# One addition and one fp32 product for a norm's sum over heads, and the second exponential of a visit ahead of its FFN group

## The chip, the cores and the metric

The kernel runs on one core of one Trainium2 chip. The metric is device microseconds of one launch. Most runs of a kernel agree within about 0.3%. A timed run is about 1.8 us longer than the span of its profile, which goes from the first to the last instruction.

## The reference

Blockwise causal attention on `q, k, v` of shape (8, 8, 576, 64), then an RMS norm and a SwiGLU FFN on the 4608 tokens of 512 features:

```python
attn = softmax(scale * q @ k.T, masked by blocks of 64)        # per head
x    = (attn @ v) with heads side by side                      # 4608 x 512
rms  = sqrt(mean(x * x, axis=-1) + 1e-06)
xn   = x / rms * rms_g
g, val = xn @ w_gate, xn @ w_val                               # 512 -> 1536
out  = (g * (1 / (1 + exp(-g))) * val) @ w_out                 # 1536 -> 512
```

## The kernel before

It treats attention batch by batch and lays the FFN's groups between attention's steps, in the order in which the program was written, so that TensorE always has products to do.

**An FFN group** (up). Eight products fill two PSUM buffers, ScalarE takes a tanh of the first, and VectorE makes `gs` and then `HT`. The buffer of `g` comes free with `gs`, that of `u` with `HT`. All FFN groups, norms and value products share four such buffers, in turn.

```python
g = ps_f.tile([P, TOKC], FP32, name="fps")        # ps_f has 4 buffers
u = ps_f.tile([P, TOKC], FP32, name="fps")
...                                               # 4 + 4 matmuls of 128x512 (line 502)
nc.scalar.activation(out=th, in_=g, func=AF.Tanh, scale=0.5)                    # line 506
nc.vector.scalar_tensor_tensor(out=gs, in0=th, scalar=1.0, in1=g, ...)          # line 508
nc.vector.tensor_mul(out=HT[n][:, m:m + k, lo:lo + w], in0=gs..., in1=u...)     # line 510
```

**The norm** of a batch, as a chain of small VectorE operations on 18 columns: a transpose `tr`, reciprocal, two products `w`, then for batches 2 to 7 the sum over heads, split into three bf16 terms whose products with a constant matrix are added in PSUM. A chain of nine more operations (from `ve`), the product `S` and a transpose give the spread norm `st`.

```python
nc.vector.tensor_add(out=rest[:, 0:n], in0=w2[:, 0:n, 0], in1=w2[:, 0:n, 1])   # line 388
for i in range(3):
    nc.vector.tensor_copy(out=term[:, i, 0:n], in_=rest[:, 0:n])               # line 391, a cast
    if i < 2:
        nc.vector.tensor_sub(out=rest[:, 0:n], in0=rest[:, 0:n], in1=term[:, i, 0:n])
...
for i, x in enumerate(terms):
    nc.tensor.matmul(ms[:, 0:n], GSUM if len(terms) == 2 else GSUMB, x, ...)   # line 401
```

**A visit** to attention, batches 3 to 7: two scores products (each into one of two PSUM buffers), the value products of pairs that are complete, and between one and three FFN groups. The number of groups is 1 in only four visits, all in batch 3. I number batch 3's visits from 0; those four are 0, 2, 4 and 6.

```python
es = [scores_mm(*x) if x[2] is not None else scores_ends_mm(x[0]) for x in two]
if len(complete) > 1:
    values_of_two()
...
for n in range(max(1, int(want) - given)):
    if es:
        scores_exp(*es.pop(0))
    group()
    given += 1
for e in es:
    scores_exp(*e)
```

**Corners.** Causal blocks need a 64 x 64 corner of an exponential set to zero. `scores_exp` notes it, and `clear()` at the end of `group()` writes the zeros.

The softmax here doesn't subtract the row's maximum and nothing guards it: scores larger than these inputs give would overflow.

Of the kernel before, what the change touches and what calls it, by code (L numbers as in the profile page):

```python
# [9 lines left out]
FP32 = mybir.dt.float32  # L10
BF16 = mybir.dt.bfloat16
# [6 lines left out]
def kernel(  # L18
# [11 lines left out]
    nc = tc.nc  # L30
# [4 lines left out]
    P = 128  # L35
# [6 lines left out]
    NSUB = S // 32  # L42
# [25 lines left out]
    const = ctx.enter_context(tc.tile_pool(name="const", bufs=1))  # L68
# [8 lines left out]
    small = ctx.enter_context(tc.tile_pool(name="small", bufs=1))  # L77
# [19 lines left out]
    SEL = const.tile([P, 7, 32], BF16, name="SEL")  # L97
    SELB = const.tile([P, HP, P], BF16, name="SELB")
    GSUM = const.tile([P, P], FP32, name="GSUM")
    GSUMB = const.tile([P, P], BF16, name="GSUMB")  # L100
    gscale = const.tile([P, HP], FP32, name="gscale")


# [68 lines left out]
    for t in range(HP):  # L172
        for a in range(2):
            r = 32 * t + a
            nc.vector.tensor_copy(out=SELB[:, t, a * D:(a + 1) * D],
                                  in_=ident[:, r:r + 1].to_broadcast([P, D]))
# [3 lines left out]
    for i in range(4):  # L180
        nc.gpsimd.affine_select(
            out=GSUM.rearrange("p (j i) -> p j i", j=4), in_=GSUM.rearrange("p (j i) -> p j i", j=4),
# [41 lines left out]
    def clear():  # L224
        while corners:
            nc.vector.memset(corners.pop(0)[1], 0.0)
# [9 lines left out]
    def scores_mm(b, t, step):  # L236

        if step in (0, "a"):
            PT[b, t] = ppool.tile([P, 2, PW], BF16, name="PT")
        sp = ps_s.tile([P, 2, 512], FP32, name="sps")  # L240
        for c, q0, w, o in STEPS[step][0]:
            for a in range(2):
                r = slice(a * D, (a + 1) * D)
                nc.tensor.matmul(sp[:, a, o:o + w], KT[b][r, t, c * P:(c + 1) * P],  # L244
                                 QT[b][r, t, q0:q0 + w], start=True, stop=True,
                                 skip_group_check=True)
        return (b, t), sp, step

    def scores_exp(pair, sp, step):

        if step is None:
            nc.scalar.activation(out=P4[pair].rearrange("p a t d -> p a (t d)"),
                                 in_=sp[:, :, 0:HP * BLK], func=AF.Exp, scale=SCALE)
            return
        parts, lo, width = STEPS[step]
        pt = PT[pair]
        nc.scalar.activation(out=pt[:, :, lo:lo + width], in_=sp[:, :, 0:width],  # L257
                             func=AF.Exp, scale=SCALE)
        for c, q0, w, o in parts:
            if c and q0 == c * P:  # L260
                corners.append((pair, pt[BLK:P, :, lo + o:lo + o + BLK]))
# [66 lines left out]
    nrm = {}  # L328
# [42 lines left out]
            o += w  # L371
        nrm[key] = tr, o

    def norm_ratio(key, split=False):
        tr, width = nrm[key]
        n = width // 32
        tv = tr.rearrange("p (s r) -> p s r", r=32)
        rec = small.tile([P, NSUB, 2], FP32, name="rec")
        nc.vector.reciprocal(out=rec[:, 0:n], in_=tv[:, 0:n, 0:2])
        w2 = small.tile([P, NSUB, 2], FP32, name="w2")  # L380
        nc.vector.tensor_mul(out=w2[:, 0:n], in0=tv[:, 0:n, 2:4], in1=rec[:, 0:n])
        nc.vector.tensor_mul(out=w2[:, 0:n], in0=w2[:, 0:n], in1=rec[:, 0:n])
        if not split:
            nrm[key] = (rec, [w2[:, 0:n, 0], w2[:, 0:n, 1]], n)
            return

        rest = small.tile([P, NSUB], FP32, name="ws")
        nc.vector.tensor_add(out=rest[:, 0:n], in0=w2[:, 0:n, 0], in1=w2[:, 0:n, 1])
        term = small.tile([P, 3, NSUB], BF16, name="wt")
        for i in range(3):  # L390
            nc.vector.tensor_copy(out=term[:, i, 0:n], in_=rest[:, 0:n])
            if i < 2:
                nc.vector.tensor_sub(out=rest[:, 0:n], in0=rest[:, 0:n], in1=term[:, i, 0:n])
        nrm[key] = (rec, [term[:, i, 0:n] for i in range(3)], n)

    def norm_root(key):

        rec, terms, n = nrm[key]
        ms = ps_f.tile([P, 512], FP32, name="fps")
        for i, x in enumerate(terms):  # L400
            nc.tensor.matmul(ms[:, 0:n], GSUM if len(terms) == 2 else GSUMB, x,
                             start=(i == 0), stop=(i == len(terms) - 1))
        ve = small.tile([P, NSUB], FP32, name="ve")
        nc.vector.tensor_scalar_add(out=ve[:, 0:n], in0=ms[:, 0:n], scalar1=EPS)
        sh = small.tile([P, NSUB], I32, name="sh")
        nc.vector.tensor_single_scalar(sh[:, 0:n], ve[:, 0:n].bitcast(I32), 1,
                                       op=ALU.logical_shift_right)
        y = small.tile([P, NSUB], FP32, name="y0")
        nc.vector.tensor_scalar(out=y[:, 0:n].bitcast(I32), in0=sh[:, 0:n], scalar1=-1,
                                scalar2=0x5f3759df, op0=ALU.mult, op1=ALU.add)  # L410
        nrm[key] = (rec, ve, y, n)
# [102 lines left out]
    def ffn_down(n, i):  # L514
        eng = nc.gpsimd if n < NTC - 2 else nc.sync
        rows = []
        for j in range(2):
            blk = (n * TOKC + i * P) // BLK + j
            b, pos = divmod(blk, S // BLK)
            rows.append(b * S + ((pos + 1) % (S // BLK)) * BLK)  # L520
        osb = obuf.tile([P, DM], FP32, name="osb")
        last = (n, i) == downs[-1]
        step = DM // 2 if last else DM
        for o in range(0, DM, step):
            po = ps_f.tile([P, DM], FP32, name="fps")
            for m in range(NMC):
                nc.tensor.matmul(po[:, 0:step], HT[n][:, m, i * P:(i + 1) * P],  # L527
                                 WO[:, m, o:o + step], start=(m == 0), stop=(m == NMC - 1))
            nc.scalar.mul(out=osb[:, o:o + step], in_=po[:, 0:step], mul=0.5)  # L529
            if rows[1] == rows[0] + BLK:  # L530
                eng.dma_start(out=out[rows[0]:rows[0] + P, o:o + step], in_=osb[:, o:o + step])  # L531
            else:
                for j in range(2):
                    e = nc.scalar if last and j else eng
                    e.dma_start(out=out[rows[j]:rows[j] + BLK, o:o + step],  # L535
                                in_=osb[j * BLK:(j + 1) * BLK, o:o + step])
# [19 lines left out]
    def group(n=1):  # L556

        nonlocal ui, di, gone
        for _ in range(n):
            dn, dt = downs[di] if di < len(downs) else (0, 0)  # L560
            have = NMC * (dn + 1) if dn or dt > 1 else NMC // 2
            ready = di < len(downs) and have <= ui
            up = ui < len(ups) and ups[ui][0] * TOKC + ups[ui][3] + ups[ui][4] <= ready_x
            far = ui - NMC
            if ready and have + 2 <= ui and far >= DOWN0 and (ui == len(ups) or 3 * di <= far - 3):
                ffn_down(*downs[di])
                di += 1
            elif up:
                ffn_up(*ups[ui])
                ui += 1  # L570
            elif ready:
                ffn_down(*downs[di])
                di += 1
            clear()
            gone += 1
            now = [d for d in due if d[0] <= gone]
            due[:] = [d for d in due if d[0] > gone]
            for _, fn, args in now:
                fn(*args)
# [18 lines left out]
    def late_tail(b):  # L598
        norm_sums(b, b, WHOLE)
        norm_squares(b, b, WHOLE)  # L600
        norm_turn(b)
        norm_ratio(b, True)
        later(2, norm_root, b)
        later(2, norm_newton, b, 0)
        later(3, norm_newton, b, 1)
        later(3, norm_spread, b)
        later(3, norm_copies, b)
        for t in range(HP):
            later(9 + t // 2, norm_apply, b, t)
        later(10, mark, b * S + S)  # L610
# [79 lines left out]
    later(2, norm_newton, "b", 1)  # L690
    later(2, norm_spread, "b")

    nc.vector.tensor_copy(out=GSUMB, in_=GSUM)


    group()
    transpose_pair(1, 0, on_act="qk")
# [73 lines left out]
    want = given = 0  # L771
# [12 lines left out]
    for i in range(0, len(steps), 2):  # L784
        two = steps[i:i + 2]
        if sums:
            late_tail(sums.pop())
# [3 lines that stand above are left out]
        complete += [x[0:2] for x in two if x[2] == 2]  # L791
        b = two[0][0]
        want += 10 / 6.5 if b == 3 else 16 / 6.5
        for n in range(max(1, int(want) - given)):
            if es:
                scores_exp(*es.pop(0))
            group()
            given += 1
        for e in es:
            scores_exp(*e)  # L800
        fetch(b + 1, 2)
    group()
    values_of_two()
# [34 lines left out]
```

## Time and profile before

| | before |
|---|---|
| median of all runs at the prediction | 392.32 us (392.03 to 392.41) |
| span of the profile | 392.3 us |
| TensorE busy, VectorE busy, ScalarE busy | 95%, 68%, 48% |
| small operations of a split, each from start to start | 0.21 us |

TensorE sets the time, so a change elsewhere counts only where TensorE waits. The views are shown in the prediction (the number in brackets is idle time before the line, with what ended it). This profile had a slow start. Here TensorE waits for batch 0's values at 14 us (the number in brackets is idle time before the line, with what ended it):

```profile
15.92 0.22 PE L299 MATMUL fps<-PT,VB 128*64 128x64 bf16 x2 [1.49 <-DMA VB<-in_v_dram]
```

The trace also shows the clock granted to TensorE at half from 16.12 to 19.53 us; the changed kernel's trace shows no such stretch at the start. The profiled run took 394.07 us, 1.8 above the median of the timed ones. So two profiles can be compared only from a common point behind the start. I use the end of the fourth output copy on ScalarE, at 78.51 us in this trace.

### The profile page before, as it was taken

How to read it: one execution, taken by the hardware profiler on the slowest of the kernel's cores; microseconds unless marked ns; L12 is line 12 of the kernel's file. 1: busy time of each engine (PE TensorE's matmuls, PEld its weight loads, DVE VectorE, ACT ScalarE, POOL GpSimd, SP SyncE). 2: the span in 40 equal slices, each digit the busy share in tenths (PEclk: the TensorE clock that was granted, in tenths of full speed). 3: DMA queues.
4: the chain of work that ended last, by engine and by line, in shares of the span. 5: the costliest groups of instructions: out<-in, count | busy, mean ns of one | idle time of the engine just before them, and what ended most of it. 6: DMA issues, size and time to landing. Idle time of an engine off the chain costs nothing.

```text
span 392.3 us, 7763 instructions
## 1 busy us (share of the span) xinstructions
PE 374.6 (95%) x3017; PEld 182.4 (46%) x3056; DVE 265.1 (68%) x651; ACT 189.6 (48%) x270; POOL 128.7 (33%) x181
## 2 busy tenths in 40 slices
PE   7779999999999999999999999999999999999996
PEld 3457666433434444444444444444444444444443
DVE  4678668377887788368977686488776847554430
ACT  3733883277555645465566445546542323332322
POOL 8826864756117402494030742400100110100000
PEclk9899999999999999999999999999999999999999
DMA  7999999999919918999961999802100220100113
GB/s 99 166 203 195 184 154 156 154 178 164 166 38 112 133 22 139 166 113 137 134 102 11 78 179 160 131 1 74 42 15 29 67 89 29 27 27 28 53 34 102
DMA packets 143364, 40.11 MB, mean 102 GB/s; under 512 B 129504, under 2 KB 140640, under 8 KB 143328
## 3 DMA queue, kind: packets, MB, share of 16 engines
q0 software_dynamic: 108448, 26.75, 69.3%
q1 hardware_dynamic: 34192, 12.74, 19.7%
q8 instruction: 24, 0.39, 0.4%
q10 hardware_dynamic: 688, 0.13, 0.2%
q14 instruction: 12, 0.10, 0.1%
HBM read 41.75 MB, written 10.17 MB: 132 GB/s over the span
## 4 chain that ended last, share of the span: by engine, by line
PE 81%; DVE 10%; ACT 2%; DMA 2%; issue 2%; POOL 2%; DVEq 0%; POOLq 0%
PE fps L502 43%; PE fps L527 23%; PE fps L299 6%; PE sps L244 5%; DVE HT L510 3%; PE fps L339 2%; DMA VB<-in_v_dram 2%; DVE gs L508 2%; ACT PT L257 1%; POOL nt L112 1%; DVE tr L370 1%; ACT th L506 1%; DVE OT L321 1%; PE fps L454 1%; DVE SQ L325 1%
## 5 line engine op out<-in xcount | busy, mean ns | idle before, releaser
L502 PE MATMUL fps<-XT,WG 128*128 128x512 bf16 (+1 forms) x466 | 110.6, 358 | 3.0 <-DVE HT L510 1.9
L508 DVE SCALAR_TENSOR_TENSOR gs<-th,fps 128x512 bf16<-128x512 f32 x108 | 74.0, 685 | 57.2 <-ACT th L506 56.2
L502 PE MATMUL fps<-XT,WV 128*128 128x512 bf16 (+1 forms) x467 | 109.5, 357 | 0.6
L257 ACT ACTIVATE PT<-sps 128x1024 bf16<-128x1024 f32 (+1 forms) x96 | 93.4, 990 | 24.0 <-PE sps L244 23.9
L506 ACT ACTIVATE th<-fps 128x512 f32<-128x512 f32 x108 | 64.7, 599 | 66.1 <-PE fps L502 65.1
L527 PE MATMUL fps<-WO,HT 128*128 128x512 bf16 (+1 forms) x434 | 96.1, 373 | 0.5
L510 DVE TENSOR_TENSOR HT<-gs,fps 128x512 bf16<-128x512 bf16 x108 | 74.3, 688 | 11.6 <-DVE gs L508 0.5
L502 PEld LDWEIGHTS <-WV 128*128 128x128 bf16 x480 | 46.9, 98 | 47.0 <-issue 1.1
L502 PEld LDWEIGHTS <-WG 128*128 128x128 bf16 x480 | 43.4, 98 | 50.0 <-issue 11.3
L527 PEld LDWEIGHTS <-HT 128*128 128x128 bf16 x444 | 42.8, 98 | 49.5 <-issue 1.7
L529 ACT ACTIVATE osb<-fps 128x512 f32<-128x512 f32 (+1 forms) x37 | 21.7, 586 | 75.7 <-PE fps L527 68.5
L531 POOL DMA_DIRECT2D out_dram<-osb x22 | 12.6, 574 | 134.2 <-ACT osb L529 130.0
L126 POOL DMA_DIRECT2D VB<-in_v_dram x48 | 39.7, 848 | 4.5 <-PE fps L312 2.4
L244 PE MATMUL sps<-QT,KT 64*128 64x192 bf16 (+5 forms) x280 | 31.5, 311 | 3.3 <-ACT PT L257 1.3
L119 POOL DMA_DIRECT2D nt<-in_k_dram x30 | 26.3, 878 | 6.9 <-DMA WO<-in_moe_w_out_dram 3.0
L119 POOL DMA_DIRECT2D nt<-in_q_dram x30 | 26.4, 880 | 4.4 <-DMA VB<-in_v_dram 3.4
L299 PE MATMUL fps<-PT,VB 128*64 128x192 bf16 (+5 forms) x280 | 25.8, 315 | 1.6 <-DMA VB<-in_v_dram 1.5
L535 POOL DMA_DIRECT2D out_dram<-osb x12 | 6.5, 548 | 57.8 <-ACT osb L529 57.8
L299 PEld LDWEIGHTS <-VB 128*64 128x64 bf16 x344 | 15.2, 112 | 13.4 <-issue 6.1
L321 DVE CAST OT<-fps 128x512 bf16<-128x512 f32 (+1 forms) x34 | 19.0, 562 | 2.0 <-PE fps L299 1.8
L244 PEld LDWEIGHTS <-KT 64*128 64x128 bf16 x280 | 9.4, 94 | 22.4 <-issue 17.0
L483 DVE SCALAR_TENSOR_TENSOR XT<-OT,gscale,bc 128x576 bf16<-128x576 bf16 (+2 forms) x24 | 15.7, 714 | 2.8 <-DMA bc<-rows 2.7
(74 smaller groups left out, 205.8 us busy)
## 6 DMA issues: line engine op xcount, KB each, us to landing
out_dram<-osb POOLq DMA_DIRECT2D x22, 256.0 KB, 2.5
VB<-in_v_dram POOLq DMA_DIRECT2D x32, 128.0 KB, 6.0
nt<-in_q_dram POOLq DMA_DIRECT2D x24, 128.0 KB, 6.4
nt<-in_k_dram POOLq DMA_DIRECT2D x24, 128.0 KB, 6.6
bc<-rows SPq DMA_DIRECT2D x10, 288.0 KB, 4.8
WG<-in_moe_w_gate_dram POOLq DMA_DIRECT2D x4, 384.0 KB, 10.0
WV<-in_moe_w_val_dram POOLq DMA_DIRECT2D x4, 384.0 KB, 11.2
WO<-in_moe_w_out_dram POOLq DMA_DIRECT2D x4, 384.0 KB, 7.8
```

What stands on the lines that cost most here:

```text
L119: nc.gpsimd.dma_start(out=nt[0:rows, 0:512].rearrange("p (h d) -> p h d", h=H), in_=src[b, :, c * P:c * P + rows, :].rearrange("h p d -> p ...
L126: nc.gpsimd.dma_start(out=vb[r:r + n, cc, :].rearrange("p (h d) -> p h d", h=H), in_=v[b, :, tok:tok + n, :].rearrange("h p d -> p h d"))
L244: nc.tensor.matmul(sp[:, a, o:o + w], KT[b][r, t, c * P:(c + 1) * P], QT[b][r, t, q0:q0 + w], start=True, stop=True, skip_group_check=True)
L257: nc.scalar.activation(out=pt[:, :, lo:lo + width], in_=sp[:, :, 0:width], func=AF.Exp, scale=SCALE)
L299: nc.tensor.matmul(ov[a * D:(a + 1) * D, o:o + w], vb[:, c, h * D:(h + 1) * D], rhs, start=(i == 0), stop=(i == len(chunks) - 1), skip_gro ...
L321: nc.vector.tensor_copy(out=o, in_=i)
L502: nc.tensor.matmul(acc[:, i * w:(i + 1) * w], wt[c][:, p, r * P:(r + 1) * P], XT[:, p, x0:x0 + w], start=(p == 0), stop=(p == HP - 1), ski ...
L506: nc.scalar.activation(out=th, in_=g, func=AF.Tanh, scale=0.5)
L508: nc.vector.scalar_tensor_tensor(out=gs, in0=th, scalar=1.0, in1=g, op0=ALU.add, op1=ALU.mult)
L510: nc.vector.tensor_mul(out=HT[n][:, m:m + k, lo:lo + w], in0=gs.rearrange("p (k w) -> p k w", k=k), in1=u.rearrange("p (k w) -> p k w", k=k))
L527: nc.tensor.matmul(po[:, 0:step], HT[n][:, m, i * P:(i + 1) * P], WO[:, m, o:o + step], start=(m == 0), stop=(m == NMC - 1))
L529: nc.scalar.mul(out=osb[:, o:o + step], in_=po[:, 0:step], mul=0.5)
```

## The change

It has two parts: less work for VectorE in the norm, and scores buffers that come free sooner in visits with one group.

```diff
-    def norm_ratio(key, split=False):
+    def norm_ratio(key, fold=False):
 ...
-        rest = small.tile([P, NSUB], FP32, name="ws")
-        nc.vector.tensor_add(out=rest[:, 0:n], in0=w2[:, 0:n, 0], in1=w2[:, 0:n, 1])
-        term = small.tile([P, 3, NSUB], BF16, name="wt")
-        for i in range(3):
-            nc.vector.tensor_copy(out=term[:, i, 0:n], in_=rest[:, 0:n])
-            if i < 2:
-                nc.vector.tensor_sub(out=rest[:, 0:n], in0=rest[:, 0:n], in1=term[:, i, 0:n])
-        nrm[key] = (rec, [term[:, i, 0:n] for i in range(3)], n)
+        ws = small.tile([P, NSUB], FP32, name="ws")
+        nc.vector.tensor_add(out=ws[:, 0:n], in0=w2[:, 0:n, 0], in1=w2[:, 0:n, 1])
+        nrm[key] = (rec, [ws[:, 0:n]], n)
 ...
-            nc.tensor.matmul(ms[:, 0:n], GSUM if len(terms) == 2 else GSUMB, x,
-                             start=(i == 0), stop=(i == len(terms) - 1))
+            nc.tensor.matmul(ms[:, 0:n], GSUM, x, start=(i == 0), stop=(i == len(terms) - 1))
 ... (the bf16 constant GSUMB and its cast go too)
-        for n in range(max(1, int(want) - given)):
-            if es:
-                scores_exp(*es.pop(0))
+        n = max(1, int(want) - given)
+        given += n
+        scores_exp(*es[0])
+        if n == 1:
+            for e in es[1:]:
+                scores_exp(*e)
             group()
-            given += 1
-        for e in es:
-            scores_exp(*e)
+        else:
+            group()
+            for e in es[1:]:
+                scores_exp(*e)
+            group(n - 1)
```

More of the change, by code (lines that the diff above doesn't have):

```diff
@@ L99 @@
     GSUM = const.tile([P, P], FP32, name="GSUM")
-    GSUMB = const.tile([P, P], BF16, name="GSUMB")
     gscale = const.tile([P, HP], FP32, name="gscale")
@@ L382, in norm_ratio @@
         nc.vector.tensor_mul(out=w2[:, 0:n], in0=w2[:, 0:n], in1=rec[:, 0:n])
-        if not split:
+        if not fold:
             nrm[key] = (rec, [w2[:, 0:n, 0], w2[:, 0:n, 1]], n)
             return
-        rest = small.tile([P, NSUB], FP32, name="ws")
-        nc.vector.tensor_add(out=rest[:, 0:n], in0=w2[:, 0:n, 0], in1=w2[:, 0:n, 1])
-        term = small.tile([P, 3, NSUB], BF16, name="wt")
-        for i in range(3):
-            nc.vector.tensor_copy(out=term[:, i, 0:n], in_=rest[:, 0:n])
-            if i < 2:
-                nc.vector.tensor_sub(out=rest[:, 0:n], in0=rest[:, 0:n], in1=term[:, i, 0:n])
-        nrm[key] = (rec, [term[:, i, 0:n] for i in range(3)], n)
+        ws = small.tile([P, NSUB], FP32, name="ws")
+        nc.vector.tensor_add(out=ws[:, 0:n], in0=w2[:, 0:n, 0], in1=w2[:, 0:n, 1])
+        nrm[key] = (rec, [ws[:, 0:n]], n)
     def norm_root(key):
@@ L691 @@
     later(2, norm_spread, "b")
-    nc.vector.tensor_copy(out=GSUMB, in_=GSUM)
     group()
```

## The prediction

> **What bounds the kernel now.** I read the page's busy shares first, then the chain of work that ended last, then TensorE's own waits, then the timeline around each norm and each late wait.
>
> ```profile
> PE 374.6 (95%) x3017; PEld 182.4 (46%) x3056; DVE 265.1 (68%) x651; ACT 189.6 (48%) x270; POOL 128.7 (33%) x181
> ...
> PE 81%; DVE 10%; ACT 2%; DMA 2%; issue 2%; POOL 2%; DVEq 0%; POOLq 0%
> ```
>
> TensorE is busy 374.6 of 392.3 us and carries 81% of the chain. The change takes almost nothing off TensorE, so all it can win is time in which TensorE stands still. VectorE carries 10% of the chain: it is not the bound, but TensorE meets it in places. The list of TensorE's waits names them (waited for, us in total, times, longest):
>
> ```profile
> PE fps L502 <- DVE HT L510: 1.9, 5, 0.6
> PE sps L244 <- ACT PT L257: 1.3, 3, 0.5
> PE fps L454 <- DVE st L432: 0.7, 2, 0.4
> ```
>
> The first row is an FFN group waiting for a PSUM buffer until VectorE's last product (HT) of an earlier group has read it. The second is the scores product waiting for the exponential that still reads its PSUM buffer. Both are what the change aims at. The timeline around the last batch's norm shows the first:
>
> ```profile
> 301.16 0.18 DVE L388 TENSOR_TENSOR ws<-w 128x18 f32<-128x18 f32 x1
> 301.38 0.18 DVE L391 CAST wt<-ws 128x18 bf16<-128x18 f32 x1
> ...
> 302.23 0.18 DVE L391 CAST wt<-ws 128x18 bf16<-128x18 f32 x1
> 302.31 0.68 DVE L508 SCALAR_TENSOR_TENSOR gs<-th,fps 128x512 bf16<-128x512 f32 x1
> 302.52 0.10 PEld L401 LDWEIGHTS <-GSUMB 128*128 128x128 bf16 x1
> 303.05 0.22 PE L401 MATMUL fps<-wt,GSUMB 128*128 128x18 bf16 x3 [0.15 <-DVE gs L508]
> ...
> 303.10 0.69 DVE L510 TENSOR_TENSOR HT<-gs,fps 128x512 bf16<-128x512 bf16 x1
> ...
> 303.84 1.02 PE L502 MATMUL fps<-XT,WG 128*128 128x512 bf16 x4 [0.57 <-DVE HT L510]
> ```
>
> VectorE goes through its queue in order. Its five splitting operations (three casts, two subtractions, one each 0.21 us) stand ahead of gs, whose tanh had been ready since 300.94. gs starts at 302.31, HT ends at 303.79, and TensorE's next group starts at 303.84.
>
> The exponentials' wait in a visit with one group:
>
> ```profile
> 129.79 0.60 ACT L506 ACTIVATE th<-fps 128x512 f32<-128x512 f32 x1 [0.16 <-PE fps L502]
> ...
> 130.28 1.02 ACT L257 ACTIVATE PT<-sps 128x1024 bf16<-128x1024 f32 x1
> ...
> 131.35 0.40 PE L244 MATMUL sps<-QT,KT 64*128 64x320 bf16 x4 [0.44 <-ACT PT L257]
> ```
>
> The second exponential waits behind the group's tanh, which waits for the group's first product. It ends at 131.30, and the second scores product of the next visit starts at 131.35.
>
> **What the Trainium skill says.** "VectorE: DVE Perf Modes", section "Rules for kernel authors", advises for chained operations: "Minimize op *count*, not sems". The trace agrees: an addition over 18 elements lasts 178 ns and the next starts 0.21 us after it, so 31 removed operations are worth removing for their count alone. "SBUF — State Buffer", section "Who interferes with whom", says that casts in a two-port mode can be locked out by GpSimd for a whole instruction, while a product of two tensors is only in the way of GpSimd's reads. Three of the 18 casts took 0.59 to 0.63 us instead of 0.18, and each ends within 10 ns of a GpSimd DMA issue (180.25, 224.11, 224.99): it agrees, and the addition that stays was 178 to 180 ns in all six. "TensorE: Matmul & The Clock Gate", section "Weight-path perf modes", leaves fp32 out of the fast weight load: here a weight load took 190 ns in fp32 and 96 ns in bf16. It says in its table of specifications that ScalarE's queue is strictly first in, first out; that is what the exponential behind the tanh shows.
>
> **The change part by part.** I measure a stall of TensorE from start to start. A 512-column product starts 0.216 us after the one before when nothing holds it; what exceeds that, or the usual gap between two such lines elsewhere, is a stall. (Idle times read smaller, because ends are modelled.)
>
> Fold, on VectorE. Each of six norms (batches 2 to 7) loses five operations at 0.21 us, 1.07 us, plus the 0.4 to 0.9 us of the slow casts in batches 4 and 5. One cast of the constant (0.42 us at 34.75) goes too, but gs after it starts at 35.08 with its tanh ready at 35.05: nothing. In all 7 us leave VectorE; only what TensorE waited for counts:
> - Batch 2: products of L401 0.06, two waits for buffers at 109.92 (0.11) and 110.97 (0.19), and 0.49 at 115.85 where L454 waits for the spread norm st: 0.85 us.
> - Batch 3: none; two scores and a down group follow, which need no buffer in time.
> - Batch 4: 0.11 + 0.64 (182.11) + 0.11: 0.86 us.
> - Batch 5: 0.13 + 0.12: 0.25 us.
> - Batch 6: 0.33 (262.83) + 0.11: 0.44 us.
> - Batch 7: 0.31 + 0.64: 0.95 us.
>
> Sum 3.35 us. Does it all go? In batch 7 gs would start at 301.34 + 0.02, HT end at 302.85, and TensorE reaches the norm product at 302.73 and the next group at 302.88: just gone. In batch 4 the tanh (179.42) now sets gs, HT ends at 180.9 against a need at 181.36: gone.
>
> Fold, on TensorE. The three bf16 products occupy 0.155 us from start to the next line's start (109.125 to 109.279). The first norms use the fp32 form already: two products, each seen as two passes, took 0.363 us (72.125 to 72.488), with passes 0.112 apart and the first hidden to 0.028. One product is then 0.14 us. Six of them save 0.09 us, which is nothing.
>
> Exponentials. The instruction order changes only for the four visits with one group, all in batch 3. The first is followed by norm sums and shows no wait. The other three show excesses of 0.31 (112.43), 0.67 (124.32) and 0.60 us (131.35). In the first and third the second exponential now ends 0.8 to 1.2 us earlier, before TensorE asks. In the middle one ScalarE is behind anyway (a copy until 122.04, two exponentials until 123.85, need at 123.65), so 0.47 go. Sum 1.38 us. The price is a tanh later by about an exponential: HT of the middle visit ends at 125.9 instead of 124.86, and TensorE needs its buffer at about 126.8.
>
> At batch 2 both parts meet: st comes 1.07 us earlier and L454 can't start before it, while the parts promise 0.85 + 0.31. So 0.1 is counted twice. Total 3.35 + 1.38 + 0.09 - 0.1 = 4.7 us, or 387.6 us.
>
> **The rivals.**
> - Given back later: a TensorE that arrives earlier meets the next wait (DMA of the norm rows, VectorE's backlog, the tanh). For it: VectorE is busy 35.0 of the 45 us from 260 to 305, and the norm's root chain of nine small operations stays ahead of gs. Against: after 305 TensorE runs almost without idle time, with VectorE at 44 of 87 us, so what is won before flows to the end. It would leave half: 390 us.
> - The fp32 product is the new cost: its weights take twice as long, and if neither pass hides, 6 x 0.38 = 2.3 us come back, 390 us. Against: the measured 0.112 us per pass in the same kernel.
> - The later tanh takes the place of the exponential's wait: HT late, the next group without a PSUM buffer. It would cost the 1.4 us of that part and leave 389 us. The margins above (0.7 us and more) speak against.
> - VectorE bound throughout, so that all 7 us count: 385 us. Against: VectorE is 68% busy and batch 3's norm shows no stall at all.
>
> **Range and chances.** I take a tenth of the gain as given back, 4.3 us, and predict 388.0 us. With half the gain lost it is 390; with all of it and some waits that I counted short, 386.8. Range 386.8 to 390.2. The edge of 2% is 384.5 us, beyond even the rival that counts all of VectorE's time, so faster has 0.03, within 2% 0.96, slower 0.01 (only a mistake in a chain of buffers could do that).
>
> **What would show it.** In the changed profile TensorE's waits on HT should fall from 1.9 us to under 0.5, and its waits on the exponential from 1.3 to about 0.3, left at the middle visit. VectorE's busy time should fall by about 7 us, with all six additions at 0.18 us. The fp32 product should take about 0.14 us from its start to the next line's. TensorE's busy time should hardly move. Of the gain, 3.2 us should be at the norms and 1.3 between 109 and 132 us. It is wrong if TensorE still idles at L502 after the norm product, if L454 at batch 2 still waits for st by more than 0.4 us, or if new waits on HT follow the single-group visits.

## The result and the profile after

| | before | after |
|---|---|---|
| median | 392.17 us (391.98 to 392.41, 4 runs) | 389.16 us (389.02 to 389.30, 4 runs) |
| ratio, 95% interval | | 0.9923 (0.9906 to 0.9940) |
| span of the profile | 392.3 us | 387.5 us |

A ratio is the mean time of one kernel's fast runs over that of the other's of the same rounds, so not quite the ratio of the medians. The time lies in the predicted range, but 1.2 us above the predicted 388.0: 3.0 us gained where 4.7 were added up and 4.3 predicted. These are the rows of TensorE's own waits in the changed kernel that matter here (waited for, us in total, times, longest):

```profile
PE fps L446 <- DVE st L424: 0.8, 2, 0.4
PE sps L243 <- ACT PT L256: 0.6, 2, 0.4
...
PE fps L494 <- DVE HT L502: 0.5, 2, 0.3
...
PE fps L298 <- DVE PT L225: 0.4, 1, 0.4
```

(Lines moved: 494 is the FFN product, 502 HT, 256 the exponential, 424 st, 225 the corner's zeros.) The FFN's wait for HT fell from 1.9 us to 0.5 and the scores' wait for the exponential from 1.3 to 0.6; what is left of both lies outside the norms and visits that were changed (on HT at 28.7 and 35.0 us, on the exponential at 16.8 and 78.1). The wait for st has not fallen at all, and the last row is new: a value product waits for a corner's zeros.

Where was the time won? For each trace I took the ends of ScalarE's copies of output tiles, subtracted those of the kernel before, and then took the difference from one point to the next. (Negative: this stretch became shorter, in us.) The columns are named by what lies in them, with times of the trace before:

| stretch | 78.5 to 119.7: batch 2's norm, visits 0 to 3 | 119.7 to 148.2: visits 4 to 7, batch 3's norm | 148.2 to 199.4: batch 4's norm | 199.4 to 229.4: batch 5's | 229.4 to 280.1: batch 6's | 280.1 to 309.0: batch 7's | sum |
|---|---|---|---|---|---|---|---|
| expected by the prediction's terms | -1.06 | -1.07 | -0.86 | -0.25 | -0.44 | -0.95 | -4.6 |
| changed kernel | -0.54 | -0.12 | -0.87 | -0.18 | -0.45 | -0.97 | -3.13 |

(The prediction's 0.09 us for TensorE is not spread over the columns.) After 309 us no further difference arises, in any kernel below. The sum is close to the 3.0 us of the timed runs; the other 1.6 us between the two spans arose before 78.5 us, at the slow start.

Four columns are as predicted. Batch 7 shows how: `gs` now stands right behind the addition, with no split between them. It starts 0.31 us after its tanh ended (297.18), where it was 1.37 us in the kernel before. HT ends at 298.97, and the next group starts 0.14 us behind the norm's product, with no idle time in brackets.

```profile
297.40 0.18 DVE L386 TENSOR_TENSOR ws<-w 128x18 f32<-128x18 f32 x1
297.49 0.68 DVE L500 SCALAR_TENSOR_TENSOR gs<-th,fps 128x512 bf16<-128x512 f32 x1
298.28 0.69 DVE L502 TENSOR_TENSOR HT<-gs,fps 128x512 bf16<-128x512 bf16 x1
...
298.97 0.29 PE L394 MATMUL fps<-ws,GSUM 128*128 128x18 f32 x2
299.11 1.02 PE L494 MATMUL fps<-XT,WG 128*128 128x512 bf16 x4
```

The first two columns lack 1.5 us. There the exponential order was changed, and the new wait lies there. This is VectorE at visit 6, in the kernel before:

```profile
130.42 0.69 DVE L508 SCALAR_TENSOR_TENSOR gs<-th,fps 128x512 bf16<-128x512 f32 x1 [0.67 <-ACT th L506]
131.21 0.69 DVE L510 TENSOR_TENSOR HT<-gs,fps 128x512 bf16<-128x512 bf16 x1
131.95 0.19 DVE L226 MEMSET PT<- 64x64 uint32 x2
```

And ScalarE, VectorE and TensorE there in the changed kernel:

```profile
127.20 1.02 ACT L256 ACTIVATE PT<-sps 128x1024 bf16<-128x1024 f32 x1
...
128.10 0.60 ACT L498 ACTIVATE th<-fps 128x512 f32<-128x512 f32 x1
128.22 0.58 PE L243 MATMUL sps<-QT,KT 64*128 64x448 bf16 x6
...
128.74 0.69 DVE L500 SCALAR_TENSOR_TENSOR gs<-th,fps 128x512 bf16<-128x512 f32 x1 [0.94 <-ACT th L498]
...
129.53 0.69 DVE L502 TENSOR_TENSOR HT<-gs,fps 128x512 bf16<-128x512 bf16 x1
130.27 0.19 DVE L225 MEMSET PT<- 64x64 uint32 x2
130.44 0.41 PE L298 MATMUL fps<-PT,VB 128*64 128x320 bf16 x4 [0.42 <-DVE PT L225]
```

The scores no longer wait. But the tanh now starts behind the second exponential, VectorE stands idle for it for 0.94 us, and the corner's zeros, queued behind `gs` and HT, come 0.42 us too late for the value product.

My theory A was therefore: the fold earns what it should, and the exponential order earns nothing net, because the tanh that it delays holds back zeros behind it, and because zeros that now come one group earlier stand in batch 2's norm chain. Rival B: the exponentials earn their 1.4 us, and the fold less than I counted (through the fp32 product, say).

### The profile page after: what moved, and what is told of

Read it like the earlier page. It is cut to its first block, busy times and chain, and to the rows that moved or that the text cites. A ratio compares the mean times of both kernels' runs of the same rounds, so it can differ in the third digit from the quotient of the medians.

```text
span 387.5 us, 7757 instructions
## 1 busy us (share of the span) xinstructions
PE 375.6 (97%) x3050; PEld 182.7 (47%) x3050; DVE 259.7 (67%) x620; ACT 189.3 (49%) x270; POOL 128.6 (33%) x181
## 4 chain that ended last, share of the span: by engine, by line
PE 86%; DVE 8%; ACT 4%; issue 1%; DVEq 0%
PE fps L494 45%; PE fps L519 24%; PE sps L243 5%; PE fps L298 5%; PE fps L338 3%; DVE HT L502 2%; ACT PT L256 2%; DVE gs L500 2%; PE fps L147 1%; ACT th L498 1%; PE fps L201 1%; DVE XT L439 1%; PE fps L446 1%; PE fps L360 0%; ACT KT L206 0%
## 5 line engine op out<-in xcount | busy, mean ns | idle before, releaser
L494 PE MATMUL fps<-XT,WV 128*128 128x512 bf16 (+1 forms) x480 | 111.0, 358 | 0.1
```

Of the source, the lines that this page charges most:

```text
L494: nc.tensor.matmul(acc[:, i * w:(i + 1) * w], wt[c][:, p, r * P:(r + 1) * P], XT[:, p, x0:x0 + w], start=(p == 0), stop=(p == HP - 1), ski ...
```

## The experiments

Each kernel gave a correct result. Their stretches, made as in the table above:

| kernel | 78.5 to 119.7 | to 148.2 | to 199.4 | to 229.4 | to 280.1 | to 309.0 | sum |
|---|---|---|---|---|---|---|---|
| changed kernel | -0.54 | -0.12 | -0.87 | -0.18 | -0.45 | -0.97 | -3.13 |
| fold_only | -0.60 | +0.07 | -0.87 | -0.18 | -0.45 | -0.97 | -2.99 |
| exp_only | +0.51 | -0.19 | -0.01 | 0.00 | 0.00 | 0.00 | +0.30 |
| late_clear | -1.05 | -0.27 | -0.87 | -0.18 | -0.45 | -0.97 | -3.79 |
| early_clear | -0.52 | -1.00 | -0.87 | -0.17 | -0.45 | -0.97 | -3.99 |
| mixed_clear | -1.06 | -1.00 | -0.87 | -0.18 | -0.45 | -0.97 | -4.53 |
| fp32_product_only | -0.01 | +0.07 | -0.01 | +0.06 | 0.00 | -0.01 | +0.09 |
| split_by_max | 0.00 | 0.00 | -0.41 | -0.24 | +0.01 | 0.00 | -0.65 |
| one_bf16_product | -0.72 | -0.05 | -0.98 | -0.29 | -0.54 | -1.06 | -3.65 |

Where nothing was changed, a stretch repeats to 0.01 us, so the trace tells apart what the timed runs hardly can.

### fold_only: the exponentials in the old order

```diff
-        n = max(1, int(want) - given)
 ... (the visit's loop of the changed kernel)
+        for n in range(max(1, int(want) - given)):
+            if es:
+                scores_exp(*es.pop(0))
+            group()
+            given += 1
+        for e in es:
+            scores_exp(*e)
```

> The fold alone, exponentials in the old order. Theory A (the new exponential order earns nothing net: the tanh that it delays holds VectorE's queue, and the corner memsets that it moves stand in batch 2's norm chain): at least as fast as the changed kernel, about 388.9 us, 3.3 us under the kernel before; in the trace the norm of batch 2 gains about 0.85 us where the changed kernel gained 0.59, batches 4 to 7 gain 2.4 to 2.5 as there. Rival B (the exponential order earns its 1.4 us, and the fold less than I counted): 390.5 us.

Measured: 389.42 us (388.92 to 389.53, 5 runs), ratio 0.9920 (0.9908 to 0.9932). The fold is nearly the whole gain, and B falls. It was not faster than the changed kernel, as I had expected by 0.3 us, but 0.14 us slower in the trace. Batch 2 gained 0.60 and not 0.85: with VectorE ahead, TensorE comes earlier to visit 3's scores and waits there for the exponential instead. From start to start that wait is 0.47 us, where it was 0.28 in the kernel before; the other 0.07 us is the fp32 product ahead of scores (0.225 us against 0.155). The waits for the exponential grew from 1.3 us in 3 places to 1.8 in 5; of the two new ones, 0.30 us at 110.8 is the one at visit 3, and 0.18 at 17.0 belongs to the start:

```profile
PE sps L243 <- ACT PT L256: 1.8, 5, 0.5
```

### exp_only: the new order, the split kept

```diff
 (the kernel before, with the visit's loop of the changed kernel)
```

> The new exponential order alone, the split kept. Theory A: no gain, 392.0 to 392.6 us, as two memsets now stand in batch 2's VectorE chain (+0.3 each) and the waits on the exponential turn into waits on corner memsets and buffers. Rival B: 390.8 us.

Measured: 392.68 us (392.20 to 392.79, 5 runs), ratio 1.0004 (0.9992 to 1.0015): no gain. The trace splits it in +0.51 us at batch 2 and -0.19 at visits 4 to 7. The scores' wait for the exponential fell to 0.6 us; in its place stand these two, which were 0 and 0.7 us in the kernel before. Of the first row only 0.42 us, at 131.4, is at a visit; the other 0.83, at 15.2, belongs to the start. The second row grew by the wait at batch 2, from 0.33 to 0.81:

```profile
PE fps L299 <- DVE PT L226: 1.3, 2, 0.8
PE fps L454 <- DVE st L432: 1.2, 2, 0.8
```

### late_clear: the second exponential's corners cleared one group later

```diff
         if n == 1:
+            known = len(corners)
             for e in es[1:]:
                 scores_exp(*e)
+            held = corners[known:]
+            del corners[known:]
             group()
+            corners.extend(held)
```

> The changed kernel with the corners of the second exponential cleared one group later, which gives VectorE the order of the fold alone; ScalarE keeps the new order. Theory A, part on the memsets: batch 2's spread norm comes about 0.5 us earlier, and the whole takes about 388.7 us; the wait of the values product at 130.4 stays, as those corners are of the first exponential. If the memsets' place is harmless: 389.1 us as the changed kernel.

Measured: 388.53 us (388.06 to 390.77, 6 runs), ratio 0.9910 (0.9888 to 0.9931). Batch 2's stretch gained another 0.51 us. VectorE's order is now exactly that of fold_only, so the two differ by the order of the exponentials alone, which there is worth 1.05 - 0.60 = 0.45 us. The place of two memsets is what had eaten it, one each from visits 0 and 2. The second of them, in the changed kernel, on VectorE and with the TensorE line that waits:

```profile
111.77 0.69 DVE L502 TENSOR_TENSOR HT<-gs,fps 128x512 bf16<-128x512 bf16 x1
112.52 0.11 DVE L225 MEMSET PT<- 64x64 uint32 x1
112.65 0.20 DVE L421 TENSOR_TENSOR S<-rec,y 128x36 bf16<-128x36 f32 x1
112.88 0.78 DVE L424 STREAM_TRANSPOSE st<-S 128x576 bf16<-128x576 bf16 x1
...
113.71 0.59 PE L446 MATMUL fps<-st,SELB 128*128 128x512 bf16 x2 [0.39 <-DVE st L424]
```

And with the memset one group later:

```profile
111.46 0.69 DVE L502 TENSOR_TENSOR HT<-gs,fps 128x512 bf16<-128x512 bf16 x1
112.07 0.19 DVE L421 TENSOR_TENSOR S<-rec,y 128x36 bf16<-128x36 f32 x1
112.30 0.78 DVE L424 STREAM_TRANSPOSE st<-S 128x576 bf16<-128x576 bf16 x1
...
113.13 0.59 PE L446 MATMUL fps<-st,SELB 128*128 128x512 bf16 x2
```

From HT's start to that of S it is 0.88 us with the memset and 0.61 without: a memset that lasts 0.11 us costs the chain 0.27. The other 0.24 us had arisen before this HT: the memset of visit 0 stood in front of the norm's first transpose. Without it S starts 0.08 us before HT's record ends; with it the memset starts 0.07 us after HT's end. This agrees with a rule of the Trainium skill, "VectorE: DVE Perf Modes", section "Two Vector instructions with no wait between them": an instruction whose output starts in another group of 32 partitions than the last output into the same memory starts only when all earlier Vector instructions have finished. The corners start at partition 64, everything around them at 0. The rest of the changed kernel's trace fits: none of the 39 corner memsets right behind an HT starts before that record's end (0.05 to 0.07 us after it), while 42 of the 44 right behind another corner memset, which starts at the same partition, start 0.04 us before its end. But no run here was made to isolate the rule. TensorE's idle time ahead of L446, 0.39 us in the changed kernel, is gone.

As expected, the wait of the value product stayed (0.4 us, once).

### early_clear: corners cleared ahead of the group

```diff
         if n == 1:
             for e in es[1:]:
                 scores_exp(*e)
+            clear()
             group()
```

> The changed kernel with all corners cleared before the FFN group of a single-group visit, ahead of that group's two VectorE operations. Theory A, part on the values product: its wait for the corner memset (0.42 us idle at 130.4) is gone, 0.5 us; batch 2 about as in the changed kernel; 388.7 us. If the wait only moves to the next instruction: 389.1 us.

Measured: 388.56 us (388.36 to 388.76, 4 runs), ratio 0.9900 (0.9887 to 0.9913). Visits 4 to 7 gained 1.00 us instead of 0.12, nearly the 1.07 of the prediction. VectorE writes the zeros in the time in which it waited for the tanh:

```profile
127.58 0.26 DVE L225 MEMSET PT<- 64x64 uint32 x3
128.18 0.60 ACT L498 ACTIVATE th<-fps 128x512 f32<-128x512 f32 x1
...
128.81 0.69 DVE L500 SCALAR_TENSOR_TENSOR gs<-th,fps 128x512 bf16<-128x512 f32 x1 [0.96 <-ACT th L498]
...
129.51 0.79 PE L298 MATMUL fps<-PT,VB 128*64 128x512 bf16 x8
```

The tanh is as late as in the changed kernel, VectorE waits for it as long, and it costs nothing. So not the late tanh itself took the gain, but what was queued behind it. I had expected 0.5 us more than the changed kernel; it was 0.86 in the trace. From start to start the value product's wait had been 0.59 us (0.78 in the changed kernel, 0.19 here). Another 0.27 us is an FFN product at 124.89 in the changed kernel, whose PSUM buffer waited for four small VectorE operations behind the delayed HT and three memsets; with the zeros ahead of the group, that excess is gone too.

### mixed_clear: late in visits 0 and 2, early in visits 4 and 6

In the loop `i` is twice the visit's number.

```diff
         if n == 1:
+            known = len(corners)
             for e in es[1:]:
                 scores_exp(*e)
+            held = corners[known:] if i < 8 else []
+            if held:
+                del corners[known:]
+            if i >= 8:
+                clear()
             group()
+            corners.extend(held)
```

> The changed kernel with the second exponential's corners cleared late in the first two single-group visits (beside batch 2's norm) and all corners cleared ahead of the group in the last two. If the two gains are of different places they add: 0.5 us at batch 2 and 0.85 us between 118 and 148 us, so 387.8 us, the fastest so far. If they are one gain seen twice: 388.5 us, as either alone.

Measured: 387.81 us (387.28 to 390.03, 6 runs), ratio 0.9893 (0.9875 to 0.9911). The two gains add, stretch by stretch, to 4.53 us: the prediction's sum but for 0.2 us. It has the lowest median and the largest gain in the traces of all the kernels here, although the interval of its ratio overlaps those of late_clear and early_clear. Its profile fell on the run of 390.03 us, with a start 2.1 us later than the changed kernel's profile (waits for batch 0's values again, and the clock at half from 18.09 to 21.50 us); from 78.5 us on it is as in the table.

### fp32_product_only: one fp32 product, all of VectorE's operations kept

```diff
-            nc.vector.tensor_copy(out=term[:, i, 0:n], in_=rest[:, 0:n])
+            nc.vector.tensor_copy(out=term[:, i, 0:n], in_=(rest if i else ws)[:, 0:n])
 ... (rest starts from ws in the same way; same operations, results unused)
-        nrm[key] = (rec, [term[:, i, 0:n] for i in range(3)], n)
+        nrm[key] = (rec, [ws[:, 0:n]], n)
```

> The kernel before with the one fp32 product fed from the sum, while VectorE still does all five splitting operations (their result is not used). If VectorE's operation count is the whole of the fold's gain: no gain, 392.2 to 392.5 us, with the waits for HT at batches 4, 6 and 7 as before, and 0.07 us lost where scores follow the product. If the product itself matters: up to 2 us faster, 390.2 us.

Measured: 392.26 us (391.93 to 392.60, 4 runs), ratio 1.0000 (0.9987 to 1.0013). No gain: the fold's gain is VectorE's five operations. The sum is there five operations, some 1 us, ahead of the split's last term, and it does not help: at batch 7 TensorE still waits for `gs` and HT behind the split:

```profile
301.09 0.40 PE L403 MATMUL fps<-ws,GSUM 128*128 128x18 f32 x2
301.14 0.69 DVE L512 TENSOR_TENSOR HT<-gs,fps 128x512 bf16<-128x512 bf16 x1
...
301.88 1.02 PE L504 MATMUL fps<-XT,WG 128*128 128x512 bf16 x4 [0.39 <-DVE HT L512]
```

### split_by_max: the casts as a two-input operation

```diff
-            nc.vector.tensor_copy(out=term[:, i, 0:n], in_=rest[:, 0:n])
+            nc.vector.tensor_tensor(out=term[:, i, 0:n], in0=rest[:, 0:n],
+                                    in1=rest[:, 0:n], op=ALU.max)
```

> The kernel before with its three splitting casts written as a maximum of the sum with itself, a two-input operation, to the same bf16 values. If GpSimd's DMA issues lock out only the casts: all 18 take about 0.18 us, batch 4 gains 0.42 us and batch 5 up to 0.2 us, 391.7 us. If any VectorE operation there is blocked: three slow ones stay and the time is 392.2 us.

Measured: 391.78 us (391.49 to 392.56, 4 runs), ratio 0.9990 (0.9975 to 1.0004): the timed runs don't settle it, the trace does. In batches 4 and 5, minimum, median and maximum in ns, in the kernel before:

```profile
L391 DVE CAST wt<-ws x6: 177/388/627, 179.2 to 224.4; 128x18 bf16<-128x18 f32 x6
```

and with the maximum:

```profile
L391 DVE TENSOR_TENSOR wt<-ws x6: 177/178/178, 177.8 to 222.1; 128x18 bf16<-128x18 f32 x6
```

No operation is slow any more, while GpSimd goes on issuing transfers beside them. The stretches of batches 4 and 5 gained 0.41 and 0.24 us, the others nothing. So the skill's page on SBUF, cited in the prediction, agrees, and about half of the fold's gain at batch 4 was the lockout of one cast rather than the number of operations.

### one_bf16_product: the sum rounded to bf16

```diff
 (fold_only, with)
-        ws = small.tile([P, NSUB], FP32, name="ws")
+        ws = small.tile([P, NSUB], BF16, name="ws")
 ... (and the product with the bf16 constant)
```

> The fold with the sum rounded to bf16 and one bf16 product, exponentials in the old order (less exact on purpose): VectorE as in the fold alone, TensorE with one quick product. From the 0.225 us (before scores) and 0.140 us (before FFN groups) of the fp32 product in the trace, I expect about 0.105 and 0.03 us instead, 0.5 to 0.7 us in six norms: 388.7 to 388.9 us against 389.4 us of the fold alone. If the fp32 product's passes were hidden anyway: 389.4 us.

Measured: 388.76 us (388.38 to 389.15, 4 runs), ratio 0.9911 (0.9898 to 0.9923). Against fold_only it gains 0.66 us over six norms, about 0.1 each. From the product's start to the next line's it is 0.106 us before scores (fp32 0.225) and 0.03 to 0.05 before FFN groups (fp32 0.140). It rounds the mean of squares to bf16's 8 bits of mantissa, so it is no fair replacement, but it puts a price on the fp32 form.

## Why the prediction was right or wrong

**The bound and the anchor.** Right: TensorE's busy time hardly moved (374.6 us with 3017 recorded products, 375.6 with 3050), and only waits counted. VectorE's operations sum to 6.9 us less, but the busy time of the page fell by only 5.4, since records of operations that follow without a gap overlap by some 0.1 us; there my sign of 7 us named the wrong view.

**The fold at batches 4 to 7.** Right, site by site: 0.86, 0.25, 0.44 and 0.95 predicted, 0.87, 0.18, 0.45 and 0.97 measured. Reading the stalls from start to start, and checking for each that the next limit lies behind it, was worth the trouble. fp32_product_only shows that it is VectorE's operations, split_by_max that 0.65 us of it was the slow casts.

**The fp32 product.** The 0.14 us was right where an FFN group follows, and wrong where scores of 64 rows follow: 0.225 against the 0.155 of three bf16 products. That is 0.07 us lost at batches 2, 3 and 5 instead of 0.015 gained. It explains the 0.07 us that batch 5 lacks. The rival of a costly fp32 product was right in direction and 2.3 us was far too much.

**The double count at batch 2.** The term was 1.06 us with both parts, and late_clear measured 1.05. The changed kernel got 0.54. The sum was right but for one thing that I had before me in the instruction order and did not price: the new exponential order brings the corners' zeros of visits 0 and 2 one group forward, into the norm's chain. Taking them out gives the 0.51 us back. So one of the prediction's own signs of being wrong came true, a wait for st of more than 0.4 us at batch 2: from start to start it is 0.55 us in the changed kernel (0.39 as idle time), 0.49 in the one before and 0.03 in late_clear.

**The exponentials.** This is the step that failed. The prediction said that the later tanh has as its price that "HT of the middle visit ends at 125.9 instead of 124.86, and TensorE needs its buffer at about 126.8", and of the rival in which the later tanh takes the place of the wait that "the margins above (0.7 us and more) speak against". The margins were those of the FFN's PSUM buffers only. Other things stand behind the same HT in VectorE's strict order: the corners' zeros, which the value product of the next visit needs, and four small products that hold a buffer of their own. With these, visits 4 to 7 gained 0.12 us where 1.07 were expected (0.19 if the 0.07 us of the fp32 product at batch 3 is left out). early_clear leaves the tanh late, moves the zeros alone, and 1.00 us is there. So the rival that I put aside was the one that came, through a door that I had not looked at.

**The size.** 4.7 us were added up, 3.13 measured in the trace. The difference of 1.6 us is 0.5 at batch 2, 0.95 at the visits, and 0.1 or so in the fp32 product. The tenth that I took off for a gain given back later stood for no measured thing: nothing was given back after 148 us, in any kernel. The measured time lies in the range because the range was wide, with room for half the gain lost to that other cause; in this the prediction was lucky.

What stays open: why some casts beside a GpSimd issue are fast (one at 180.50 took 0.18 us), and whether the 0.27 us of a memset come from its start partition, which the trace supports and no experiment tested.

## What to carry to other kernels

When one engine's operation is made later to free another's buffer sooner, list everything that is queued behind it on its engine, not just the buffer that it frees: here two memsets that last 0.19 us together, behind a late product, took back 0.59 us of gain. Such small operations belong where their engine waits anyway, and out of a serial chain in which the next engine waits for the end. In this kernel TensorE's waits could be summed to a tenth of a microsecond from start-to-start times, where each sum had been checked against what the next limit would be.

## What the Trainium skill lacked or had wrong

- "TensorE: Matmul & The Clock Gate" has no time for an fp32 product. "FP8 and Floating Point Precision", section "TensorE Precision Notes", says that true fp32 takes four passes; the trace records two matmuls of 18 columns for each such product (how they make up four passes no run shows), and the whole takes 0.140 us ahead of FFN products and 0.225 ahead of scores, against 0.03 to 0.05 and 0.106 us for one bf16 product.
- "VectorE: DVE Perf Modes", section "Two Vector instructions with no wait between them", says what is held but not what it costs: a memset from partition 64 on, 0.11 us long, between two operations from partition 0 on lengthened the chain by 0.27 us.
- "SBUF — State Buffer", section "Who interferes with whom", agrees with the trace, but no page gives the size for an operation this small: casts of 18 columns took up to 0.63 us instead of 0.18, until within 10 ns of the end of a DMA issue on GpSimd, and the same values by a two-input maximum took 0.18 us in all 18 cases.
